# Four retention chunks in place of six ahead of the feature blocks, and every later chunk two groups further on

## The chip, the cores and the metric

The kernel runs on one core of a Trainium2 chip. The metric is the device time of one execution in microseconds (us). Lower is better.

Engine names as in the profile: PE is TensorE's matmul, PEld its weight load, DVE is VectorE, ACT is ScalarE, POOL is GpSimd, SP is the engine that issues most transfers.

## The reference, cut to what matters

```python
# retention: batch 4, 8 heads, 768 steps, head width 64
for t in range(S):
    state = gamma * state + einsum('bhd,bhe->bhde', k[:, :, t], v[:, :, t])
    y[:, :, t] = scale * einsum('bhd,bhde->bhe', q[:, :, t], state)
x = y.transpose(0, 2, 1, 3).reshape(3072, 512)
# feed-forward: 512 -> 2048 -> 512, weights arrive as float64
h = x @ w_in
g = h * erf(softplus(h))
out = g @ w_out
```

## The kernel before

The retention runs in 24 chunks of 128 steps, six to each of the four sequences. A chunk has seven parts: `K_` scales its keys and queries (DVE, later POOL), `T` transposes them on PE (ACT copies the result), `S_` multiplies keys by queries on PE, `M` masks the scores on DVE, `O_` computes the output on PE (ACT copies it into x), `U` computes the state's increment on PE and issues the load of chunk j + 3, and `A` adds the increment on DVE. There is one `U` and `A` less at the end of each sequence, and no product with the state at its start.

The feed-forward goes by groups. Groups 0 to 3 handle the first 512 tokens (chunks 0 to 3): each has four hidden blocks `hidden(g, u)`, then the activation `gate` on ACT, the product `gated` on DVE and four projection tiles `project`. Groups 4 to 23 handle 256 tokens per pair of groups with Strassen-like products (seven block products in place of eight, at the cost of sums on DVE), and each early one of them carries one retention chunk.

The weights come as float64 in 16 pieces, which DVE (with one square on ACT) turns into float32 while groups 0 to 3 use them:

```python
def conversion(n):                       # one piece: six DVE steps
    ...
    nc.vector.tensor_scalar(top, hi, 3, 0x3FFFFFF8, ...)              # L187
    nc.vector.scalar_tensor_tensor(top, hi, 0xC0000000, top, ...)     # L191
    nc.scalar.activation(square, square, AF.Square)
    nc.vector.tensor_scalar(low, top, 0xFF800000, ...)                # L197
    nc.vector.scalar_tensor_tensor(lowf, lo, 2.0**-52, lowf, ...)     # L199
    nc.vector.tensor_tensor(lowf, topf, lowf, op=ALU.add)             # L201
    nc.vector.scalar_tensor_tensor(to, square, F64_LEAST**2, lowf, ...)  # L203
    done.add(pieces[n])
    load_pieces_after(n)                 # the next piece for this place
```

The pieces are used in the order in0, in1, in2, in3, out0, out1, in4, in5, out2, out3, in6, in7, out4, out5, out6, out7, counted 0 to 15 here. Group g's hidden blocks need two "in" pieces, its projection two "out" pieces. `pace(n)` deals out conversion steps between the other DVE work, so DVE's order is fixed when the program is built. There are four places for raw pieces, and four pieces can be loaded at the start; later ones follow as places come free, in one queue with the chunks' loads.

```python
n_first = 6
for j in range(n_first):        # the opening
    S_(j); M(j); K_(j + 1); O_(j)
    if j + 1 < n_first: T(j + 1)
    U(j); ...
...
after = [                       # per group and hidden block: run at once, run a little later
    [
        ([(T, 6)], [(K_, 7)]),
        ([(S_, 6), (T, 7)], [(M, 6)]),
        ([(O_, 6), (U, 6), (S_, 7)], [(A, 6), (M, 7)]),
        ([(O_, 7), (U, 7)], [(A, 7), (K_, 8)]),
    ],
    [([], [])] * FG,
    [([], [])] * FG,
    [([], []), ([], [(x_sums, G0)]), ([], []), ([], [])],
]
for g in range(G0):             # groups 0 to 3
    for u in range(FG):
        ...
        hidden(g, u)
        run(after[g][u][0])
        waiting.extend(after[g][u][1])
    gate(g)
    if g:
        for tt in range(TT):
            project(g - 1, tt)
j = 2 * JPC                     # chunks 8 to 23 lie in groups 4 to 19
```

## Time and profile before

| kernel before | |
|---|---|
| median of the three runs at hand then (range) | 753.64 us (752.59 to 754.34) |
| profiled span | 752.8 us |
| PE busy | 726.2 us (96%) |
| DVE busy | 353.2 us (47%) |
| start of group 0, of group 4 | 47.6 us, 166.5 us |

From the page of the profile before: the busy time of each engine, then busy tenths in 40 slices of 18.8 us each (9 is 90% or more), for PE, for DVE, for PE's granted clock and for the DMA engines.

```profile
PE 726.2 (96%) x5260; PEld 610.7 (81%) x5260; DVE 353.2 (47%) x463; ACT 274.5 (36%) x320; POOL 32.2 (4%) x28
...
PE   7884999999999999999999999999999999999997
...
DVE  4967899975554324333243153063163152153323
...
PEclk9997999999999999999999999999999999999999
DMA  9999755102120120120220220120200000000000
```

The page says two things at once. Over the whole, PE is the bound. In the first four slices (75 us) it isn't: its digits are 7, 8, 8, 4, the clock falls in the fourth, and the DMA digits are 9. A later DVE hump, slices five to eight, is the weight conversion. The whole 26.6 us in which PE wasn't busy (752.8 - 726.2) is 4% of the span; the question is how much of it a new order can fill. Group 4's start is here that of its first product in PE's timeline, 166.53 us (166.7 from the chain of waits).

### The profile page before, as it was taken

How to read it: one execution, taken by the hardware profiler on the slowest of the kernel's cores; microseconds unless marked ns; L12 is line 12 of the kernel's file. 1: busy time of each engine (PE TensorE's matmuls, PEld its weight loads, DVE VectorE, ACT ScalarE, POOL GpSimd, SP SyncE). 2: the span in 40 equal slices, each digit the busy share in tenths (PEclk: the TensorE clock that was granted, in tenths of full speed). 3: DMA queues.
4: the chain of work that ended last, by engine and by line, in shares of the span. 5: the costliest groups of instructions: out<-in, count | busy, mean ns of one | idle time of the engine just before them, and what ended most of it. 6: DMA issues, size and time to landing. Idle time of an engine off the chain costs nothing.

```text
span 752.8 us, 11796 instructions
## 1 busy us (share of the span) xinstructions
PE 726.2 (96%) x5260; PEld 610.7 (81%) x5260; DVE 353.2 (47%) x463; ACT 274.5 (36%) x320; POOL 32.2 (4%) x28
## 2 busy tenths in 40 slices
PE   7884999999999999999999999999999999999997
PEld 6652544458699999999999999999999999999995
DVE  4967899975554324333243153063163152153323
ACT  2331554341532423424414424424334244324430
POOL 1000200001010110110110110101100000000000
PEclk9997999999999999999999999999999999999999
DMA  9999755102120120120220220120200000000000
GB/s 195 199 234 199 196 111 168 56 0 44 57 43 22 21 71 10 35 71 1 43 71 1 43 71 1 43 70 2 43 29 1 2 29 1 1 29 1 1 29 28
DMA packets 87522, 42.71 MB, mean 57 GB/s; under 512 B 76208, under 2 KB 76208, under 8 KB 87472
## 3 DMA queue, kind: packets, MB, share of 16 engines
q1 hardware_dynamic: 83920, 41.16, 23.3%
q10 hardware_dynamic: 3552, 0.80, 0.6%
q8 instruction: 41, 0.67, 0.4%
q14 instruction: 9, 0.07, 0.0%
HBM read 35.66 MB, written 6.29 MB: 56 GB/s over the span
## 4 chain that ended last, share of the span: by engine, by line
PE 90%; DVE 4%; DMA 2%; ACT 1%; issue 1%; SPq 1%; ACTq 0%; DVEq 0%
PE hp L553 34%; PE o L613 32%; PE o L496 7%; PE hp L483 7%; PE r L408 2%; PE r L355 2%; PE r L368 2%; PE r L422 1%; DMA w_out_sb<-in_moe_w_in_dram 1%; DMA kq<-in_q_dram 1%; PE r L403 1%; DVE am L380 1%; DVE w_out_sb L191 0%; SPq L96 0%; DVE w_out_sb L201 0%
## 5 line engine op out<-in xcount | busy, mean ns | idle before, releaser
L553 PE MATMUL hp<-xs,w_in_sb 128*128 128x128 f32 x1280 | 158.7, 278 | 0.0
L553 PEld LDWEIGHTS hp<-xs,w_in_sb 128*128 128x128 f32 x1280 | 150.3, 192 | 6.6 <-issue 3.2
L613 PE MATMUL o<-w_out_sb,h 128*128 128x256 f32 x640 | 141.6, 379 | 0.0
L472 DVE TENSOR_TENSOR e<-h,e 128x1024 f32<-128x1024 f32 x44 | 51.9, 1221 | 179.8 <-ACT e L453 179.8
L613 PEld LDWEIGHTS o<-w_out_sb,h 128*128 128x128 f32 x640 | 121.6, 190 | 16.5
L553 PE MATMUL hp<-xT,w_in_sb 128*128 128x128 f32 x960 | 113.7, 275 | 0.0
L553 PEld LDWEIGHTS hp<-xT,w_in_sb 128*128 128x128 f32 x960 | 111.9, 192 | 1.9 <-issue 1.0
L613 PE MATMUL o<-w_out_sb,e 128*128 128x256 f32 x480 | 111.5, 382 | 0.9 <-DVE e L472 0.9
L613 PEld LDWEIGHTS o<-w_out_sb,e 128*128 128x128 f32 x480 | 88.1, 190 | 12.5 <-DVE e L472 1.3
L452 ACT ACT_TABLE_LOAD x24 | 30.8, 1283 | 91.1 <-PE o L613 89.1
L483 PE MATMUL hp<-xT,w_in_sb 128*128 128x512 f32 x128 | 58.3, 611 | 0.0
L581 DVE TENSOR_TENSOR h<-h,hp 128x512 f32<-128x512 f32 x20 | 13.7, 687 | 86.7 <-PE hp L553 86.7
L346 POOL TENSOR_TENSOR kq<-kq,kq_s 128x1024 f32<-128x1024 f32 x15 | 30.0, 2000 | 499.8 <-DMA kq<-in_q_dram 428.5
L483 PEld LDWEIGHTS hp<-xT,w_in_sb 128*128 128x128 f32 x128 | 24.7, 197 | 29.7 <-issue 29.1
L576 DVE TENSOR_TENSOR h<-h,hp 128x512 f32<-128x512 f32 x20 | 13.8, 688 | 71.1 <-ACT h L574 71.1
L452 ACT ACTIVATE e<-h 128x2048 f32<-128x2048 f32 x22 | 42.0, 1910 | 0.2
L453 ACT ACTIVATE e<-e 128x2048 f32<-128x2048 f32 x22 | 42.0, 1910 | 0.2
L413 ACT COPY xT<-r 128x256 f32<-128x256 f32 x42 | 13.9, 375 | 73.4 <-PE r L408 73.4
L579 ACT COPY h<-hp 128x512 f32<-128x512 f32 x20 | 11.7, 586 | 70.8 <-PE hp L553 70.8
L355 PE MATMUL r<-ident,kq 128*128 128x128 f32 x168 | 24.2, 288 | 11.5 <-DVE am L380 9.4
L380 DVE TENSOR_TENSOR am<-r,causal 128x512 f32<-128x512 f32 x42 | 27.2, 683 | 16.3 <-PE r L368 15.9
L355 PEld LDWEIGHTS r<-ident,kq 128*128 128x128 f32 x168 | 20.3, 149 | 13.2 <-DVE am L380 9.6
(91 smaller groups left out, 678.4 us busy)
## 6 DMA issues: line engine op xcount, KB each, us to landing
w_out_sb<-in_moe_w_out_dram SPq DMA_DIRECT2D x14, 512.0 KB, 4.6
kq<-in_k_dram SPq DMA_DIRECT2D x24, 256.0 KB, 3.5
v<-in_v_dram SPq DMA_DIRECT2D x24, 256.0 KB, 4.9
w_in_sb<-in_moe_w_in_dram SPq DMA_DIRECT2D x12, 512.0 KB, 7.0
out_dram<-r SPq DMA_DIRECT2D x24, 256.0 KB, 2.3
kq<-in_q_dram SPq DMA_DIRECT2D x21, 256.0 KB, 4.7
w_out_sb<-in_moe_w_in_dram SPq DMA_DIRECT2D x4, 512.0 KB, 9.2
w_in_sb<-in_moe_w_out_dram SPq DMA_DIRECT2D x2, 512.0 KB, 4.0
```

The costliest lines, as they stand in the source:

```text
L346: engine.tensor_tensor(KQ[j], KQ[j], by, op=ALU.mult)
L355: nc.tensor.transpose(p[:, u, :], KQ[j][:, i, 2 * u : 2 * u + 2, :].rearrange("p h d -> p (h d)"), ident,)
L368: nc.tensor.matmul(pp[s][:, hp, :], KT[j][s * D : (s + 1) * D, hp, :], QT[j][s * D : (s + 1) * D, hp, :], start=True, stop=True,)
L380: nc.vector.tensor_tensor(AM[j][:, s], SC[j][s], causal[:, None, :].to_broadcast([P, HP, C]), op=ALU.mult)
L408: nc.tensor.matmul(place(h), V[j][:, h, :], AM[j][:, h % 2, h // 2, :], start=(not c and h % 4 < 2), stop=True, skip_group_check=True,)
L452: nc.scalar.activation(E[g], HS[g], AF.Softplus)
L453: nc.scalar.activation(E[g], E[g], AF.Erf)
L472: nc.vector.tensor_tensor(E[g][:, half], HS[g][:, half], E[g][:, half], op=ALU.mult)
L483: nc.tensor.matmul(p, w_in_of(ft, kk), XC[0][:, kk, :], start=(kk == 0), stop=(kk == n_k - 1))
L496: nc.tensor.matmul(O[0][tt].rearrange("p (d c) -> p d c", d=2), E[g][:, u * TCH + tt * P : u * TCH + (tt + 1) * P], w_out_of(ft), start=(f ...
L553: nc.tensor.matmul(bank[:, u, :], w_in_sb[:, s, IN[a], kk, u * P : (u + 1) * P], XS[m][b][:, kk, :], start=(p in (1, 2, 5) and u == 0 and ...
L613: nc.tensor.matmul(O[m][i][:, half, :], G[g][a][:, u * P : (u + 1) * P], w_out_sb[:, s, OUT[b], u, :], start=i not in started, stop=(s == ...
```

## The change

The intent: start the feature blocks as soon as their 512 tokens exist (four chunks), put chunks 4 and 5 among the blocks of groups 1 and 2, and leave group 0 free of chunks, so that PE has work that waits for no transfer. Chunks 6 and 7 go to groups 4 and 5, and every later chunk two groups on.

```diff
-    load(1)
     load_piece(0)
+    load(1)
     load(2)
@@ scaling
-        engine = nc.vector if j <= 2 * JPC else nc.gpsimd
+        engine = nc.vector if j <= JPC + 2 else nc.gpsimd
@@ loads at the end of U
-        if j >= 4:
-            load_held()
-        if j + 3 < NJ:
+        if j == 0 or JPC <= j < NJ - 3:
             load(j + 3)
@@ opening
-    n_first = 6
+    n_first = JPC
...
-        K_(j + 1)
+        if j + 1 < n_first:
+            K_(j + 1)
@@ chunks among the blocks
     after = [
+        [([], []), ([(load, 4)], []), ([], []), ([(load, 5)], [(K_, 4)])],
         [
-            ([(T, 6)], [(K_, 7)]),
-            ([(S_, 6), (T, 7)], [(M, 6)]),
-            ([(O_, 6), (U, 6), (S_, 7)], [(A, 6), (M, 7)]),
-            ([(O_, 7), (U, 7)], [(A, 7), (K_, 8)]),
+            ([(T, 4)], []),
+            ([(S_, 4), (load, 6)], [(M, 4)]),
+            ([(O_, 4), (U, 4)], [(A, 4)]),
+            ([], [(K_, 5)]),
         ],
-        [([], [])] * FG,
-        [([], [])] * FG,
-        [([], []), ([], [(x_sums, G0)]), ([], []), ([], [])],
+        [
+            ([(T, 5)], []),
+            ([(S_, 5)], [(M, 5)]),
+            ([(O_, 5), (U, 5)], [(A, 5)]),
+            ([], []),
+        ],
+        [([], []), ([], [(x_sums, G0)]), ([], [(K_, 6)]), ([], [])],
     ]
...
-    j = 2 * JPC
+    j = JPC + 2
```

In groups 4 on, the differences of x (`x_sums`) move behind the chunk's output, because each chunk now arrives just in time for them.

More of the change, by code (lines that the diff above doesn't have):

```diff
@@ L286 @@
         nc.scalar.dma_start(d_s[:, s], decay_s[s * D : s * D + 1, :].to_broadcast([P, HP]))
+    load_piece(0)
     load(1)
-    load_piece(0)
     load(2)
@@ L728 @@
         hidden_part(g, 5)
-        if g + 1 < NG and (g - G0) % 2:
-            x_sums(g + 1)
         if more:
@@ L738 @@
             j += 1
+        if g + 1 < NG and (g - G0) % 2:
+            x_sums(g + 1)
         if first:
```

## The prediction

> **What bounds the kernel now.** I read the page's forty slices first: TensorE (PE) is at 90% or more from about 84 us to the end, below that before. So only the opening can be shortened, unless the work behind it changes. I then cut the execution at the points where the chain of work changes its character and asked for each stretch's busy times:
>
> ```profile
> core 0: us, PE busy (x) PEld busy (x) DVE busy (x) ACT busy (x) POOL busy (x), PEclk, DMA share, GB/s
> 0.00:47.50 47.50, 37.67 (x444) 30.89 (x444) 31.61 (x43) 13.74 (x27) 2.17 (x13) 0.93 1.11 199
> 47.50:84.00 36.50, 25.70 (x164) 14.41 (x160) 27.33 (x28) 10.76 (x19) 2.88 (x1) 0.86 0.87 212
> 84.00:166.70 82.70, 82.70 (x198) 36.75 (x195) 79.03 (x78) 43.06 (x38) 2.38 (x1) 1.00 0.36 101
> 166.70:198.76 32.06, 31.51 (x218) 22.65 (x218) 13.49 (x15) 10.46 (x12) 1.90 (x1) 1.00 0.13 26
> 198.76:635.84 437.08, 437.08 (x3523) 402.88 (x3522) 160.96 (x244) 160.67 (x191) 22.84 (x12) 1.00 0.14 34
> 635.84:752.80 116.96, 111.51 (x728) 103.09 (x727) 40.78 (x58) 35.84 (x35) 0.00 (x0) 0.99 0.04 14
> ```
>
> The stretches are: six retention chunks; the four hidden blocks of group 0 with chunks 6 and 7 among them; the rest of the weight conversion (groups 1 to 3); group 4; fifteen groups that each carry a chunk; four that carry none. The reader is to see that DMA is full for 47.5 us and nearly so to 84, that PE is full afterwards, and that VectorE (DVE) is 79.03 of 82.70 us busy in the third stretch: a second engine close behind PE.
>
> In the second stretch PE is busy for 25.70 of 36.50 us. The waits of that stretch, and the chain of waits, say why:
>
> ```profile
> PE r L355 <- DVE am L380: 9.4, 1, 9.4
> DVE kq L346 <- DMA kq<-in_q_dram: 5.3, 2, 3.2
> ```
>
> ```profile
> 51.38 8.63 DMA kq<-in_q_dram
> 60.10 1.23 DVE kq L346
> ...
> 65.59 0.61 DVE am L380
> 66.24 1.97 PE r L355 x8
> ```
>
> Chunk 7's data lands at 60.1; the mask of chunk 6 stands behind chunk 7's scaling and a conversion in DVE's order, so chunk 7's transposes wait until 66.2. **DMA is the first bound.** The landings fit one count, worked out here: a chunk (0.79 MB) takes some 4.0 us of the full DMA, a weight piece (1.05 MB) some 3.6. Ahead of chunk 3 go chunks 0 to 2 and two pieces, 3 x 4.0 + 2 x 3.6 = 19.2, plus its own 4.0, from 1.5, plus about 2 to land: 26.7, and DVE starts chunk 3 at 27.16. For chunk 7 (seven chunks and six pieces before it) the count gives 57, and 60.1 is measured.
>
> DVE's own rate is one weight piece in 6.3 us, as its timeline shows for one of sixteen pieces:
>
> ```profile
> 120.72 0.69 DVE L187 TENSOR_SCALAR w_in_sb<-w_in_sb 128x1024 uint32<-128x1024 uint32 x1
> 121.44 1.22 DVE L191 SCALAR_TENSOR_TENSOR w_in_sb<-w_in_sb 128x1024 uint32<-128x1024 uint32 x1
> 122.58 0.69 DVE L197 TENSOR_SCALAR w_out_sb<-w_out_sb 128x1024 uint32<-128x1024 uint32 x1
> 123.30 1.22 DVE L199 SCALAR_TENSOR_TENSOR w_out_sb<-w_in_sb,w_out_sb 128x1024 f32<-128x1024 uint32 x1
> 124.56 1.22 DVE L201 TENSOR_TENSOR w_out_sb<-w_out_sb 128x1024 f32<-128x1024 f32 x1
> 125.89 1.22 DVE L203 SCALAR_TENSOR_TENSOR w_in_sb<-w_in_sb,w_out_sb 128x1024 f32<-128x1024 f32 x1
> ```
>
> A group of the conversion stage needs four pieces (25.2 us) and a gate product (2.35): 27.6 of DVE against 27.5 of PE (sixteen hidden and sixteen projection products, 13.73 us each on the chain).
>
> **What the Trainium skill says.** "DMA: Bandwidth & Descriptors", section "Issuing engines are not separate DMA queues": transfers issued from several engines run on the same 16 DMA engines, so reordering issues moves no bytes away. The trace agrees: 199 GB/s and a full share through 47.5 us with both queues. "SBUF — State Buffer", section "SBUF: two separate sides": GpSimd (POOL) and DVE take turns on a shared port pair, the loser blocking. The trace agrees in direction: a POOL scaling at 89.41 (2.38 us) meets a DVE step of 2.81 us that otherwise takes 1.22. "TensorE: Matmul & The Clock Gate", section "What's actually happening": an idle PE falls to half clock and needs a busy window to come back. The granted clock is 0.86 in the second stretch and 1.00 in the third, so fewer gaps also save some slow microseconds. "Perfetto Trace Analysis", section "Optimization Strategy": regimes with different limits may gain by interleaving; that is what this change does.
>
> **The change part by part.** *Removed from the opening:* chunks 4 and 5 with their loads, and from group 0 chunks 6 and 7. *Moved:* chunks 4 and 5 into groups 1 and 2; every chunk from 6 on two groups later, so chunks 6 to 23 lie in groups 4 to 21. *Reordered:* piece 0 ahead of chunk 1's load; the differences of x after the chunk's output. No product is added or removed. The instruction order of the changed program confirms this.
>
> *Opening.* The bytes ahead of chunk 3's scaling are the same ones, so it stays near 27.2. From there DVE and PE go as before: transposes 28.5, scores 30.3, masks to 32.8, output to 33.6, state products to about 34.4. Group 0 then starts at 34.4, where it started at 47.6. Piece 1 is converted by about 36.3 and needed at 41.3: no wait. Group 0 takes 13.8 without chunks: 48.2 (was 84.0).
>
> *Group 1* has 13.8 of hidden blocks and chunk 4. DVE in order: pieces 2 and 3 ready at 44.8 and 51.1, chunk 4 scaled at 52.3, PE wants it at 51.6 (wait 0.7). The activation of group 0 (two table loads of 1.28, two passes of 1.91) stands ahead of the copies of chunk 4's transposes on ACT, some 1.3 more. Chunk work is 4.4 with its small copy wait: group 1's hidden blocks end near 69. *Projection 0* needs pieces 4 and 5, ready at 58.6 and 69.5, the latter wanted at 70.7: ends 82.8. *Group 2* with chunk 5 (last of its sequence, no state product) ends near 101, *projection 1* near 115, *group 3* 128.6. *Projection 2* needs piece 13 at 130.3.
>
> *DVE for piece 13.* Before, from piece 5 done (89.3) to piece 13 done (148.2) took 58.9. After: less one gate product that now lies ahead (2.35), plus scaling (1.2) and masks (1.3) of chunk 5, x differences (1.5) and one more POOL meeting (1.6): 62.1. From 69.5 this gives 131.6. So projection 2 waits some 1.2 and group 4 starts at 131.6 + 12.1 (the other seven eighths of 13.8) = **143.7, against 166.7: 23.0 gained.**
>
> *Given back.* A group with a chunk averages 437.08 / 15 = 29.14, one without 24.79 (24.78 and 24.80 measured). Two more groups carry one, 6 and 7 being added to the set: chunk 6 starts a sequence (no product with the state), such a group takes 28.8, and chunk 7's takes 29.4. (28.8 - 24.8) + (29.4 - 24.8) = 8.6. In group 4 DVE is now later: it ends the last piece at about 148.5, then one add, the gate product and two weight sums (5.5) and the mask (1.3), so chunk 6's output starts near 154.5 where PE is ready at 153: 1.2 more than before. Sum: 23.0 - 8.6 - 1.2 = 13.2 off. 753.64 - 13.2 = 740.4; I take **741.0**, as hand schedules leave out small waits.
>
> **Rivals.** *DVE becomes the bound of the third stretch.* For: it is 96% busy there already, and it gets two chunks of 2.9 us each in place of idle time in the opening. Against: it starts that stretch earlier and is fed. If conversions slip by 6 us, PE waits as long and the time is 747. *Transfers come too late:* four pieces stay held until the opening ends, and one queue issues pieces and chunks in order, so a load that waits for a buffer blocks the next piece. For: DMA was full to 84 us. Against: two chunks fewer (8 us) stand ahead of piece 4, which should land near 38 and is first read at 45. If wrong, 745 to 752. *The opening shrinks by the whole idle time and DVE keeps up without POOL meetings:* PE never waits after 34.4, group 4 starts at 140 to 141, the time is 736 to 738. For: PE's sum alone allows it. Against: the margins above are 1 to 5 us. *Nothing gained, as the moved chunks only fill PE:* excluded by 11 us of idle PE in the second stretch and 10 in the first.
>
> **Range and chances.** The gain of 23 rests on two ledgers that nearly meet; an error of 3 in either moves the result by 2 to 3. Two per cent is 15.1 us, or 738.6, only 2.4 below my number, so faster by over 2% has 0.28, within 2% 0.70. Slower by over 2% would need all of the gain and 15 us more: 0.02. Range 734.5 to 748.
>
> **What would show it.** Group 0 begins at 33 to 36 us; PE waits of 1 to 3 us in group 1; DVE over 95% busy from about 30 to 148 us; the first stage-two product at 142 to 147; 8 to 9 us more from there to the end. Wrong if chunk 3 lands after 30, if a weight piece keeps DVE idle for over 2 us after 35, or if the chunks' extra cost in late groups isn't 4.0 to 4.6 each.

## The result, and the profile after

| | before | after |
|---|---|---|
| median of four runs (range) | 753.63 us (752.59 to 754.34) | 742.17 us (741.47 to 743.62) |
| profiled span | 752.8 us | 739.9 us |
| PE busy | 726.2 us | 723.5 us |
| group 0 starts | 47.6 us | 35.0 us |
| group 4 starts | 166.5 us | 144.9 us |
| group 4 to the end | 586.3 us | 595.0 us |

The ratio is 0.9851, with a 95% interval of 0.9832 to 0.9871. A ratio here is the mean time of one kernel's fast runs over that of the other's of the same rounds, so it isn't quite the ratio of the medians. The kernel is 1.5% faster, which counts as within 2%.

The same lines of the page after the change:

```profile
PE 723.5 (98%) x5260; PEld 609.1 (82%) x5260; DVE 352.4 (48%) x461; ACT 274.3 (37%) x320; POOL 34.9 (5%) x30
...
PE   7889999999999999999999999999999999999997
...
DVE  3999999955543332531631532433414424243314
...
PEclk9999999999999999999999999999999999999999
DMA  9999653021201201302202022112021000000000
```

PE's 4 in the fourth slice is a 9 now, and the clock's 7 is a 9. The number of PE instructions is the same, 5260. The span fell by 12.9 us. Of these, 10.2 are PE time without work (26.6 before, 739.9 - 723.5 = 16.4 after) and 2.7 are a lower busy time for the same instructions (726.2 - 723.5), which fits the fuller clock (its mean was 0.988 in the profiled execution before, 0.994 after). The profiles overstate the gain a little: the profiled execution before took 754.5 us, 0.9 above its median, the one after 741.67, 0.5 below. Between the medians the gain is 11.5 us.

DVE's digits are 9 from the second slice to the eighth. The busy times by stretch, after the change: opening, groups 0 to 3, the rest.

```profile
core 0: us, PE busy (x) PEld busy (x) DVE busy (x) ACT busy (x) POOL busy (x), PEclk, DMA share, GB/s
0.00:35.00 35.00, 27.53 (x316) 23.43 (x316) 21.88 (x32) 10.57 (x20) 2.15 (x13) 0.95 1.07 198
35.00:144.90 109.90, 107.34 (x357) 49.86 (x354) 106.03 (x106) 53.48 (x55) 4.21 (x2) 0.98 0.63 155
144.90:739.90 595.00, 588.62 (x4593) 535.84 (x4591) 224.50 (x325) 210.29 (x246) 28.53 (x15) 1.00 0.13 31
```

In the middle stretch both PE (107.34 of 109.90) and DVE (106.03) are nearly always busy. The two engines have met. The DMA share is 0.63 there, and DVE's longest wait for a weight piece is 0.69 us, so transfers no longer bind.

PE's waits from 35 to 180 us, after the change (total, times, longest):

```profile
PE r L355 <- DVE kq L346: 2.0, 1, 2.0
PE r L408 <- DVE am L380: 1.0, 2, 0.8
PE o L494 <- DVE w_out_sb L203: 0.3, 1, 0.3
PE r L422 <- ACT xT L413: 0.3, 1, 0.3
```

The 9.4 us wait is gone and 2.0 us for chunk 4's scaling is the longest one left. It costs more than its length. The timeline of PE in group 1 (start, duration, what, idle before and who ended it):

```profile
54.50 1.34 PE L355 MATMUL r<-ident,kq 128*128 128x128 f32 x8 [2.05 <-DVE kq L346]
55.64 5.08 PE L481 MATMUL hp<-xT,w_in_sb 128*128 128x512 f32 x8
...
61.74 3.70 PE L481 MATMUL hp<-xT,w_in_sb 128*128 128x512 f32 x8
```

Eight products of the same kind take 5.08 us just after the gap and 3.70 us a little later; the eight transposes take 1.34, against 1.04 in group 2. The granted clock was 0.71 from 55.7 to 60.7 us, and 1.00 from 60.7 to 64.0. At projection 2, where the prediction saw DVE and PE meet, the two halves of its first tile are 0.26 us apart:

```profile
130.61 1.88 PE L494 MATMUL o<-w_out_sb,e 128*128 128x512 f32 x4
132.74 1.55 PE L494 MATMUL o<-w_out_sb,e 128*128 128x512 f32 x3 [0.26 <-DVE w_out_sb L203]
```

### The profile page after: what moved, and what is told of

It is laid out like the page before. It is cut to its first block, busy times and chain, and to the rows that moved or that the text cites. A ratio compares the mean times of both kernels' runs of the same rounds, so it can differ in the third digit from the quotient of the medians.

```text
span 739.9 us, 11780 instructions
## 1 busy us (share of the span) xinstructions
PE 723.5 (98%) x5260; PEld 609.1 (82%) x5260; DVE 352.4 (48%) x461; ACT 274.3 (37%) x320; POOL 34.9 (5%) x30
## 4 chain that ended last, share of the span: by engine, by line
PE 79%; DVE 12%; DMA 4%; issue 2%; SPq 2%; ACT 1%; DVEq 0%; ACTq 0%
PE hp L551 34%; PE o L611 32%; PE r L368 3%; PE r L408 2%; PE r L355 2%; DVE w_out_sb L199 2%; DVE w_out_sb L201 2%; PE o L494 2%; DMA w_in_sb<-in_moe_w_in_dram 2%; DMA kq<-in_k_dram 2%; PE r L422 1%; DVE w_out_sb L197 1%; PE r L403 1%; DVE w_in_sb L191 1%; DMA v<-in_v_dram 1%
## 5 line engine op out<-in xcount | busy, mean ns | idle before, releaser
L346 POOL TENSOR_TENSOR kq<-kq,kq_s 128x1024 f32<-128x1024 f32 x17 | 32.7, 1925 | 534.4 <-DMA kq<-in_q_dram 469.8
```

The costliest lines, as they stand in the source:

```text
L346: engine.tensor_tensor(KQ[j], KQ[j], by, op=ALU.mult)
```

## The experiments

Theory A, as the runs were planned: PE's products are the same wherever a chunk stands, and so is DVE's work; what was gained is idle PE time in front of group 4; after the change DVE's fixed order has no slack left in groups 0 to 3, with PE's own work only a little below it. The rivals differ from run to run and are named in each expectation. "Group 4 starts" is the first Strassen-like product on PE in the trace.

| run | median us | ratio to before (95%) | group 4 starts | span |
|---|---|---|---|---|
| the changed kernel | 742.17 | 0.9851 (0.9832 to 0.9871) | 144.9 | 739.9 |
| e1_load1_first | 741.36 | 0.9836 (0.9821 to 0.9851) | 144.3 | 739.3 |
| e2_six_first | 746.48 | 0.9901 (0.9885 to 0.9917) | 146.6 | 744.9 |
| e8_six_p0first (e2 again) | 745.62 | 0.9884 (0.9853 to 0.9916) | 145.1 | 743.3 |
| e3_chunk6_in_g3 | 743.55 | 0.9867 (0.9849 to 0.9885) | 149.2 | 740.1 |
| e4_dve_more | 751.95 | 0.9976 (0.9961 to 0.9991) | 155.0 | 749.8 |
| e5_dve_less (wrong result) | 738.74 | 0.9802 (0.9779 to 0.9825) | 142.5 | 737.1 |
| e6_k4_early | 741.20 | 0.9840 (0.9819 to 0.9861) | 146.6 | 741.6 |
| e10_no_halves | 741.81 | 0.9859 (0.9840 to 0.9877) | 144.7 | 739.8 |
| e7_combined | 737.68 | 0.9783 (0.9762 to 0.9803) | 141.2 | 735.0 |
| e9_gate_later | 737.03 | 0.9783 (0.9768 to 0.9798) | 139.4 | 734.4 |

All but e5_dve_less gave the right result.

### e1_load1_first: is the reorder of the first loads worth something?

```diff
-    load_piece(0)
     load(1)
+    load_piece(0)
     load(2)
```

> The changed kernel with chunk 1's load ahead of weight piece 0 again; all else as changed. In the changed kernel VectorE waits 3.0 us for chunk 1's keys at 12.2 us and starts chunk 3's scaling at 28.06 (27.16 before). Theory A (VectorE's own order is the bound from about 15 us to 150, so an early wait on it is carried to the end): chunk 3's scaling back at 27.2, group 0 starts 0.8 to 1.0 us earlier (34.1 for 35.0), group 4 starts 0.5 to 1.0 earlier, the time is 0.5 to 1 us lower, about 741.5. Rival B (piece 0's early landing is what keeps the conversion going; the reorder pays): the conversion of piece 0 waits until 15.6 as before the change, piece 13 is ready later than 132.7, the time is 1 us or more higher.

Chunk 3's scaling did start earlier, at 27.32 us for 28.06, and group 4 at 144.3 for 144.9. Group 0 itself started at 35.4, not at the 34.1 expected; in this profile PE idled 3.3 us in the opening at two transposes, which the profile puts down to nothing it shows. The time is 0.8 us below that of the changed kernel, but the two were measured in different sessions and their intervals overlap. So the sign agrees with theory A, the size is not settled, and rival B (the reorder pays) has nothing for it. The other traces say a little more on the opening: the five runs with piece 0 first start group 0 at 35.0 to 36.0 us, the four with four chunks ahead and chunk 1's load first at 35.4 (this one), 34.6, 34.1 and 33.7. A gain in the time from it isn't shown: of two runs below that treat chunk 4's scaling alike, e6 has piece 0 first and takes 741.20 us, e10 has chunk 1 first and takes 741.81. DVE's timeline shows the trade. First the changed kernel, where the wait for chunk 1's keys is the long one:

```profile
15.23 1.23 DVE L346 TENSOR_TENSOR kq<-kq,kq_s 128x1024 f32<-128x1024 f32 x1 [3.04 <-DMA kq<-in_k_dram]
16.37 0.69 DVE L187 TENSOR_SCALAR w_out_sb<-w_out_sb 128x1024 uint32<-128x1024 uint32 x1
```

Then this run, where the same time is split over two waits:

```profile
13.22 1.23 DVE L346 TENSOR_TENSOR kq<-kq,kq_s 128x1024 f32<-128x1024 f32 x1 [1.66 <-issue]
16.09 0.69 DVE L187 TENSOR_SCALAR w_out_sb<-w_out_sb 128x1024 uint32<-128x1024 uint32 x1 [1.64 <-DMA w_out_sb<-in_moe_w_in_dram]
```

The conversion of piece 0 begins at nearly the same time, 16.37 us there and 16.09 here. Only chunk 1 is served clearly earlier here.

### e2_six_first and its repeat: which part of the change made the gain?

Six chunks in the opening as before the change; chunks 6 and 7 in groups 4 and 5 as after it. As a difference to the changed kernel (the repeat carries a misleading label: it is the same file):

```diff
-    n_first = JPC
+    n_first = JPC + 2
...
-        [([], []), ([(load, 4)], []), ([], []), ([(load, 5)], [(K_, 4)])],
-        [ ... chunk 4 ... ],
-        [ ... chunk 5 ... ],
+        [([], [])] * FG,
+        [([], []), ([(load, 6)], []), ([(load, 7)], []), ([], [])],
+        [([], []), ([], []), ([(load, 8)], []), ([], [])],
```

together with the first issue order of before and the loads of chunks 3 to 5 in the opening. Two small parts of the change stay in: POOL scales from chunk 7 on (chunk 9 before), and the differences of x stand behind the chunk's output. So it isn't quite "one part of the change alone", as the expectation has it.

> The kernel before with one part of the change alone: chunks 6 and 7 leave group 0 and go to groups 4 and 5, all later ones two groups on; six chunks stay ahead of the feature blocks and the issue order of the first loads stays. Theory A (what was gained is the idle PE time of group 0, where chunk 7 waited for its transfer; PE's work is the same wherever a chunk is put, and VectorE's too): group 0 starts at 47.6 as before but runs through in 13.8 to 61.4; pieces 2 to 5 are ready at about 53, 59, 66 and 74, always before PE asks; piece 13 at about 131, group 4 starts at 144, the time is 740 to 743, the same as the changed kernel. Rival B (the gain comes from starting the feature blocks earlier, with four chunks): group 4 starts 8 or more us later than in the changed kernel, the time is 750 or more.

> The run with six chunks ahead again, the same kernel a second time. Its 746.5 us lay 4 us above the 740 to 743 that the ledger gave; in its trace chunk 3's scaling started at 29.7 us, 2 us later than in the run with the same order of first loads (27.3), and group 4 took 34.9 us for 31.8. Theory A (the late opening was chance of that session's transfers): chunk 3's scaling at 27 to 28 this time, group 4 starts near 144.5, the time is 741 to 743. Rival C (it belongs to the kernel: VectorE is 2 us later at group 4 with six chunks ahead, and the wait there with its slow clock costs 3): again 745 to 747.5.

Both readings missed in part. Moving chunks 6 and 7 alone brings ratios of 0.9901 and 0.9884, so about 1.0 to 1.2% of the 1.5%. That is most of the gain, which speaks against rival B of the first expectation (750 us or more). But it isn't all of it, and the repeat, with 745.62 us, says that the rest belongs to the kernel, as rival C had it. In the repeat the opening was undisturbed (chunk 3's scaling at 26.95 us) and group 4 started at 145.1, as in the changed kernel; group 4 itself then took 34.9 us for 31.7. The timeline of PE there, in the repeat:

```profile
156.97 0.44 PE L408 MATMUL r<-am,v 128*64 128x128 f32 x4 [2.43 <-DVE am L380]
157.57 1.08 PE L408 MATMUL r<-am,v 128*64 128x128 f32 x12 [0.16 <-DVE am L380]
158.58 3.44 PE L553 MATMUL hp<-xs,w_in_sb 128*128 128x128 f32 x16
```

PE waits 2.43 us for chunk 6's mask (0.84 in the changed kernel), and the sixteen products after it take 3.44 us, against 2.05 for the same products in the changed kernel; the granted clock was 0.57 there. DVE starts that mask at 156.24 us; in the changed kernel it does at 154.44. A part of this delay is visible in DVE's timeline of the repeat: with two more chunks ahead in the queue, piece 3 lands later, and DVE stands still for it (the changed kernel begins piece 3 at 40.18 after 0.69 us):

```profile
47.09 0.69 DVE L187 TENSOR_SCALAR w_in_sb<-w_in_sb 128x1024 uint32<-128x1024 uint32 x1 [1.42 <-DMA w_in_sb<-in_moe_w_in_dram]
```

That is 0.7 us of the 1.8. DVE's waits that the profile lists from 12 to 157 us add up to 7.5 us in the repeat and 5.8 in the changed kernel, a difference of about the same size, but spread over waits for transfers, for PE and for nothing that the profile shows. Group 4 started at the same time in both, although group 0 started at 46.5 us in the repeat and at 35.0 in the changed kernel. So what leaving two chunks out of the opening adds isn't an earlier group 4 but a DVE that is less late in it. That the extra waits cause the lateness is read from the traces; no run takes them away alone.

### e3_chunk6_in_g3: does the place of a chunk matter?

```diff
-        [([], []), ([], [(x_sums, G0)]), ([], [(K_, 6)]), ([], [])],
+        [ ([(T, 6)], []), ([(S_, 6)], [(M, 6), (x_sums, G0)]),
+          ([(O_, 6), (U, 6)], [(A, 6)]), ([], [(K_, 7)]) ],
...
-    j = JPC + 2
+    j = JPC + 3
```

> The changed kernel, but chunk 6 in group 3 and later chunks one group further on in place of two. Theory A (a chunk costs PE about 4 us wherever it stands, so putting it later gives nothing back and takes nothing, as long as VectorE isn't late): group 4 starts 3.5 to 4 us later (148.5 to 149), one late group loses its chunk (4.0 to 4.6), PE's wait for piece 13 (0.26 us) vanishes, the time is 741 to 742.5. Rival B (VectorE is the bound of groups 1 to 3, so 2.9 us more of it ahead of group 4 cost as much again): PE waits over 2 us in front of the second half of projection 2, the time is 744 to 746.

Group 4 starts at 149.2 us, as expected, and one late group is free of a chunk. The wait for piece 13 is gone. The time is 743.55 us (its profiled execution, 741.78 us, was the fastest of the four, so the trace reads low), 1.05 above theory A's range and 0.45 below rival B's. Rival B's own sign, a wait of over 2 us in projection 2, is absent. The ratio, 0.9867, lies within the interval of the changed kernel. So the place of a chunk beyond the opening doesn't matter within what these runs resolve. With medians 1.4 us apart, a cost of that size isn't excluded either.

### e4_dve_more and e5_dve_less: how close are the two engines?

More: one step of every conversion done twice. Less: another step left out (wrong result).

```diff
+        nc.vector.tensor_scalar(low, top, 0xFF800000, None, op0=ALU.bitwise_and)
         nc.vector.tensor_scalar(low, top, 0xFF800000, None, op0=ALU.bitwise_and)
```

```diff
-        nc.vector.scalar_tensor_tensor(lowf, lo, 2.0**-52, lowf, op0=ALU.mult, op1=ALU.mult)
```

> The changed kernel with one step of each weight conversion (0.69 us, it takes the exponent bits) done twice, the result unchanged: 0.7 x 14 = 9.7 us more of VectorE from piece 0 to piece 13. Theory A (VectorE is the bound of the conversion stage, with no slack at projection 2): piece 13 ready at 140 to 142 in place of 132.7, group 4 starts 7 to 9 us later, the time is 748 to 752. Rival B (PE is the bound and the waits in front of it are chance): 2 us or less is lost, 742 to 744.

> The changed kernel with one step of each weight conversion (the 1.22 us product that puts the low bits in place) left out; the result is wrong on purpose. VectorE has some 16 us less to do by piece 13. Theory A (PE's own work is the floor, and VectorE only touches it in a few waits): the waits of PE after 35 us vanish (2.05 + 0.25 + 0.26 + 1.0) with the slow clock behind the first of them (some 1.8), group 4 starts near 140, the time is 736 to 738. Rival B (VectorE is the real bound of groups 1 to 3, so its whole saving shows): 726 to 731.

With 11.3 us more of DVE work (363.7 us busy for 352.4) the time rises to 751.95 us, 9.8 above the changed kernel: theory A's range. Group 4 starts 10.1 us later, a little more than the 7 to 9 expected. Piece 13 is ready at 141.1 us (132.7 in the changed kernel), and PE waits for it. In the trace of this run, PE in projection 2:

```profile
141.15 1.64 PE L495 MATMUL o<-w_out_sb,e 128*128 128x512 f32 x2 [2.33 <-DVE w_out_sb L204]
```

With 19.1 us less of it (333.3 us busy) the time falls only to 738.74, by 3.4. The range had been 736 to 738, so the size was slightly overrated; group 4 started at 142.5 and not near 140. One wait of 1.9 us that I had not foreseen, for ACT's copies of chunk 4's transposes, came up where DVE no longer held PE. Rival B, in which DVE's saving would all show, is out by 7.7 us. The pair is the clearest picture of the state after the change. More DVE work shows nearly in full; less of it shows little, because PE is then the bound: from 35 us to group 4 it is busy for 105.35 of 107.50 us, and DVE for 92.48.

### e6_k4_early and e10_no_halves: can the longest wait be taken away alone?

```diff
-  ([], []), ([(load, 5)], [(K_, 4)])],
+  ([], [(K_, 4)]), ([(load, 5)], [])],
```

e10 has this too, with chunk 1's load first and the masks of chunks 4 and 5 a little earlier.

> The changed kernel with chunk 4's scaling three VectorE steps earlier, so that PE doesn't wait for it (2.05 us, and a slow clock of some 1.8 after it). Theory A (VectorE has no slack up to projection 2, so the wait moves there): chunk 4's transposes start at 52.5 for 54.5, but piece 13 stays at 132.7 and PE waits 3 to 4 us for it in projection 2 in place of 0.26; group 4 starts at 145, the time is 741.5 to 743. Rival B (the wait is PE's alone): group 4 starts at 141.5, the time is 738 to 739.

> The combined version with two of its parts undone: projections tile by tile, and group 4's order on VectorE as in the changed kernel; chunk 1's load first, chunk 4's scaling and the two masks early stay. Theory A (PE's early waits are only moved as long as piece 13 and chunk 6's mask come when they do): piece 13 is ready at 130.6 to 131, PE is there at 129 and waits 1.5 to 2, and in group 4 it waits 2 to 4 us for chunk 6's mask; the time is 740 to 741.5. Rival B (the early waits were PE's alone): as the combined version, 737 to 738.5.

The times, 741.20 and 741.81 us, each lie 0.3 us outside theory A's range (below it and above it) and 2 to 3 us above rival B's: the 2.05 us and the slow clock behind it, some 3.8 us by the timeline, aren't gained. But the reason I gave is wrong in its place. The wait for chunk 4's scaling is gone in both (transposes at 52.91 and 51.88 us), and at projection 2 PE waits only 0.22 and 1.15 us; in e10's group 4 it waits 1.0 for chunk 6's mask, not the 2 to 4 expected. The wait came back one step later in the same chunk: at the scores, for ACT, whose activation of group 0 stands ahead of the copies of the transposes. In the trace of e10_no_halves:

```profile
58.19 1.18 PE L368 MATMUL r<-qT,kT 64*128 64x128 f32 x16 [1.84 <-ACT qT L361]
```

The 5.34 us for the next eight products, 3.70 elsewhere, show the slow clock again (granted 0.55 from 59 to 61 us, 0.73 from 61 to 64). In e6_k4_early the profiled execution had a late opening as well (chunk 0's scaling at 9.07 us for 5.74), so its span says less than its median.

### e7_combined and e9_gate_later: a version that beats both

e7 is e10 with two more parts: projections in halves, so that the second "out" piece is needed 5 us later, and in group 4 chunk 6's mask ahead of the gate product and of two weight sums.

```diff
-            for tt in range(TT):
-                project(g - 1, tt)
+            for us in ((0, 1), (2, 3)):
+                for tt in range(TT):
+                    project(g - 1, tt, us)
...
-        if first:
-            gated(g - 1)
         ...
             S_(j)
             M(j)
+        if first:
+            gated(g - 1)
...
-        if p in (6, 7):
-            next(last_steps, None); next(last_steps, None)
+        if p in (6, 7) and (g > G0 or p == 7):
+            for _ in range(2 if g > G0 else 4):
+                next(last_steps, None)
```

e9 also moves the activation of group 0 behind chunk 4's copies:

```diff
-        gate(g)
+            if (g, u) == (1, 0):
+                gate(0)
+        if g:
+            gate(g)
```

> A version built on theory A: chunk 1's load ahead of piece 0 again, chunk 4's scaling earlier, the projections in two halves (the first halves of all four tiles, then the second, so that piece 13 is needed 5 us later), chunk 5's mask a little earlier, and in group 4 chunk 6's mask ahead of the gate product and of two weight sums. Theory A: no wait of PE over 1 us from 35 us on, group 4 starts at 140.5 to 142, the time is 737 to 739. Rival (VectorE's order leaves another wait in group 4, because the last piece is ready at 149 whatever PE does): group 4 starts at 141 but takes 34 to 35 us for 31.8, the time is 740 to 742.

> The combined version with the activation of group 0 (6.4 us on ACT) behind the copies of chunk 4's transposes in place of ahead of them. In the combined version PE waits 1.8 us at chunk 4's scores for those copies, and the next block runs at a slow clock. Theory: that wait vanishes and VectorE keeps 2 us or more of slack at projection 2 and in group 4, so group 4 starts 1.8 to 2.8 us earlier (138.4 to 139.4 for 141.2) and the time is 734.5 to 736. Rival (VectorE takes the wait over again, at chunk 4's mask or in group 4): 737 to 738.5.

e7_combined came out as planned: group 4 at 141.2 us, 737.68 us. Against e10_no_halves it is 4.1 us faster by the medians. The traces, 4.8 us apart, show that not all of it comes from the two relaxed points. Projection 2 is 1.4 us shorter and group 4 is 1.3 shorter, which are theirs; 0.5 is a later opening in e10; and 1.65 is the slow clock, which followed the 1.84 us wait for ACT in e10 and did not follow the same wait here (the next eight products take 3.70 us). The shares aren't independent: in e10 piece 13 is ready only at 132.6 us, so a PE that came earlier would have waited longer there. Whether e7's other executions had the slow clock isn't on record. I had written that the wait itself would not be there.

e9_gate_later removes that wait, and group 4 starts at 139.4 us, 1.8 earlier, as expected. The expectation's "slow clock" behind the wait was not in e7's trace, so only the wait was there to be gained. The time is 737.03 us, not the 734.5 to 736 expected: 0.65 us less than e7 by the medians, and nothing by the ratios, which are equal. The rival was right that DVE takes it over: group 4 is 1.2 us longer than in e7. PE in group 4 of e9:

```profile
148.08 2.05 PE L551 MATMUL hp<-xs,w_in_sb 128*128 128x128 f32 x16 [1.16 <-DVE h L567]
```

DVE in the same place, where the add that PE waits for stands right behind the last conversion step:

```profile
146.20 1.23 DVE L203 SCALAR_TENSOR_TENSOR w_out_sb<-w_out_sb 128x1024 f32<-128x1024 f32 x1
147.35 0.68 DVE L567 TENSOR_TENSOR h<-h,hp 128x512 f32<-128x512 f32 x1
```

e9's ratio of 0.9783 (0.9768 to 0.9798) is clear of 2%; e7's interval reaches 0.9803 and so isn't. Both ratios are 0.7% below that of the changed kernel.

## Why the prediction was right, point by point

The time, 741.0 predicted and 742.17 measured, and the course agree; the sizes of the terms were off by 1 to 2 us in both directions. By the profiles 21.6 us were gained ahead of group 4 (23.0 predicted) and 8.7 given back after it (8.6 + 1.2 = 9.8 predicted), so the sum, 12.9 for 13.2, is nearer than its parts. That these two misses have opposite signs is luck.

- **Opening.** Predicted: chunk 3's scaling stays near 27.2, group 0 at 34.4. Measured 28.06 and 35.0. The step that failed is "the bytes ahead are the same ones, so it stays": the bytes were, but chunk 1's keys came behind piece 0 and DVE waited 3.04 us for them. With the order undone that scaling was at 27.3 in e1.
- **Group 1.** Predicted waits of 0.7 for chunk 4's scaling and 1.3 for ACT's copies. Measured 2.05 for the first and none for the second, which hid behind it; e6, e7 and e10 show it at 1.8 to 1.9 once the first is gone. The slow clock behind the gap (1.8 us by the durations of the transposes and of the eight products) was not in the sum, although the prediction had named the clock as an effect.
- **DVE's ledger.** Predicted piece 13 at 131.6, measured 132.7; DVE over 95% busy, measured 106.03 of 109.90, or 96%. Two POOL scalings each met a DVE step (2.39 us for 0.69 and 2.80 for 1.22), as counted.
- **Group 4's start.** Predicted 143.7, measured 144.9. PE came to projection 2 two microseconds later than the ledger had it, so its wait there was 0.26 and not 1.2.
- **Given back.** Predicted 8.6 for two more chunks in late groups and 1.2 more of waits in group 4. Measured from group 4 to the end: 595.0 for 586.3, or 8.7; of these, 0.45 are more waits for the mask (1.00 for 0.55). The two late groups that newly carry a chunk take 29.38 and 28.57 us for 24.79, so 4.6 and 3.8 more; the second lies just below the 4.0 that the prediction had set as a sign, and it holds the last chunk of a sequence, whose group took 28.57 before the change too. What is "given back" is work that was moved, as e3 shows.
- **The rivals.** Transfers too late: no; the DMA share is 0.63 after 35 us and the longest DVE wait for a piece there is 0.69. DVE as the bound: half right. e4 shows that it has no slack, and e5 that PE is close behind. How close isn't settled by e5's 3.4 us: e9 lies 5.1 us below the changed kernel with all of DVE's work in place. "The opening shrinks by the whole idle time and DVE keeps up" (736 to 738): not this kernel, but e7 and e9 reach it, by giving DVE's order the slack.

One belief of mine fell in the experiments: that shortening the opening is what gains. Six chunks ahead with chunks 6 and 7 moved keeps 0.66 to 0.78 of the gain.

What stays open is the worth of the load order within 1 us, whether the 3.3 us of idle PE in e1's opening belong to it, and when a short wait of PE is followed by a slow clock.

## What to carry to other kernels

When work is moved off an opening to fill an engine, keep two ledgers, one for the engine that gets the work and one for the next busiest: the gain ends where they meet. After such a change the second engine's fixed order decides, and a wait removed alone comes back at the next point where the orders meet; relax those points together. To see which engine has slack, add a little work to one and take a little away, and read the asymmetry.

## What the Trainium skill lacked or had wrong

- "TensorE: Matmul & The Clock Gate", section "What's actually happening", gives an idle window of about 3.4 us before the clock falls. Shorter gaps were enough here: 2.05 us in the changed kernel was followed by 5.08 us for products that take 3.60 to 3.70, at a granted clock of 0.71. It isn't certain either: gaps of 1.84 to 1.90 us were followed by slow products in e6 (4.59) and e10 (5.34), and by full speed in e5 and e7 (3.70). That the window runs freely, as the page says, would fit the difference; no run here shows it.
- "SBUF — State Buffer", section "SBUF: two separate sides", says that the loser of the shared port blocks. The runs agree: a DVE step of 0.69 us took 2.39 beside a POOL scaling of 2.07. POOL scalings were stretched as well, 1.90 us alone and up to 2.88 when they met a DVE step; the page covers this too, since it lets whichever engine starts second block. So nothing is lacking here.
- "Perfetto Trace Analysis", section "Optimization Strategy", says that interleaving regimes with different limits may help. It doesn't say what bounds the gain: after the interleaving here 11.3 us more DVE work cost 9.8 us and 19.1 us less gained 3.4.
- No page works out what table loads and activations that stand ahead of small copies on ACT cost PE; here 6.4 us of them held chunk 4's scores by 1.8 to 1.9 us (e5, e6, e7 and e10), and the wait was gone when they were moved behind the copies (e9).
